# The first loads of a fused adaLN, linear attention and SwiGLU kernel, shared between the SyncE and ScalarE DMA queues

## The chip, the cores and the metric

The kernel runs on one core of one Trainium2 chip. The metric is the device time of one execution in microseconds (us), lower is better. Single executions of one kernel differ by one or two us in about 840. For each run the record gives the mean granted TensorE clock of the core (1.0 is full speed).

Engines are named as the profile names them: PE is TensorE, PEld its weight loads, DVE is VectorE, ACT is ScalarE, POOL is GpSimd, SP is SyncE. A "q" after an engine (SPq, ACTq) means its instruction sequencer, which also issues DMAs.

## The reference

One transformer block over 2048 tokens of width 1024. Only the head of it matters here: the modulation vectors come from a small condition vector `c` and the matrix `w_mod`, the input is normalised, scaled and shifted, and multiplied by the key weights.

```python
mod = (silu(c) @ w_mod).reshape(1, 6, 1, -1)          # w_mod: 1024 x 6144
sa, ca, ga, sb, cb, gb = mod[:, 0], ..., mod[:, 5]
h = layernorm(x) * (1 + ca) + sa                       # x: 2048 x 1024, bf16
x = x + ga * linear_attention(h, wqkv) @ wo
h = layernorm(x) * (1 + cb) + sb
x = x + gb * swiglu(h, w_gate, w_up, w_down)
```

## The kernel before

The kernel works on 512 tokens at a time. For the first 512 it must load four tiles of `x` (128 tokens each, 256 KB), `c`, four modulation blocks and eight key pieces (256 KB each) before it has everything for the key stage of these tokens. A modulation block `wme[b][q]` is 1 MB: half `b` of the columns for the scale (`q` = 1) or the shift (`q` = 0). All loads are issued by SyncE, in the order of need:

```python
    for st in range(STC - 1):                      # x tiles 0, 1, 2
        load_x(st, nc.sync)
    nc.sync.dma_start(out=c_sb[:], in_=c_v)
    ...
    def load_mod(b, q, lo, hi):
        nc.sync.dma_start(out=wme[b][q][:, :, lo:hi], in_=wm_v[:, :, q * D + b * NB + lo:q * D + b * NB + hi])
    def load_k(cc):
        nc.sync.dma_start(out=wk[cc // 4][:, cc % 4, :], in_=wqkv_v[:, cc, D:2 * D])

    load_mod(0, 1, 0, NB)
    load_mod(0, 0, 0, NB)
    load_k(0)
    load_k(1)
    load_x(STC - 1, nc.sync)
    load_k(2)
    load_k(3)
    load_mod(1, 1, 0, NB)
    load_mod(1, 0, 0, NB // 2)
    load_k(4)
    load_k(5)
    load_mod(1, 0, NB // 2, NB)
    load_k(6)
    load_k(7)
```

The head is written out by hand, with the order on DVE, ACT and POOL kept as written (`in_order`). PE keeps program order too. `keep_warm` issues dummy matmuls that only keep PE busy.

```python
    with in_order(nc.vector, nc.scalar, nc.gpsimd):
        ...
        nc.scalar.activation(out=scT[:], in_=mod_ps[:, 0:DC], func=ACT.Silu)
        xns = [ln1_norm(*ln1_stats(0, t)) for t in range(3)]     # normalised on ACT
        pe_transpose_tile(hT, xns[0], 0, DC)
        keep_warm(spare, 3)
        pe_transpose_tile(hT, xns[1], 1, DC)
        keep_warm(spare, 2)
        mod_block(0, 1, 0, 4)
        pe_transpose_tile(hT, xns[2], 2, DC // 2)                # half copied by ACT, half by DVE
        keep_warm(spare, 4)
        for lo, hi in ((0, 1), (1, 4)):
            mod_block(0, 0, lo, hi)
            for cc in range(lo, hi):
                modulate(hT, cc, ca1T, saT, 0, H)
        k_mms(0, gs, accs, 0, 4)                                 # the first key matmuls
        xn3 = ln1_norm(*ln1_stats(0, 3), dve=True)
        pe_transpose_tile(hT, xn3, 3, DC // 2)
        ...                                                      # block 1, the other key matmuls
```

`pe_transpose_tile(..., split)` lets ACT copy the column blocks from `split` on out of the transposed tile, and DVE the blocks before it. In the built program DVE's copy of a tile waits for ACT's copy of the same tile (tile 2: ACT from 11.78 to 12.36 us, DVE from 12.40).

In the built program of the changed kernel, the first 24 DMAs that SyncE and ScalarE issue take eight completion semaphores in rotation, over both queues together; the kernel before has such a rotation too. From the ninth on, a DMA waits, **on the engine that issues it**, for the DMA eight places earlier: in that trace each of the 16 issues begins after that DMA has landed, eleven of them within 0.02 us.

Of the kernel before, what the change touches and what calls it, by code (L numbers as in the profile page):

```python
# [21 lines left out]
def kernel(  # L22
# [13 lines left out]
    nc = tc.nc  # L36
    P = nc.NUM_PARTITIONS
    _, S, D = A_x.shape
# [4 lines left out]
    DC = D // P  # L43
# [4 lines left out]
    STC = SCW // P  # L48
    NB = 512
# [11 lines left out]
    wqkv_v = A_wqkv.rearrange("(c p) n -> p c n", p=P)  # L61
# [4 lines left out]
    wm_v = w_mod.rearrange("(j p) n -> p j n", p=P)  # L66
    c_v = c.rearrange("o (j p) -> (o j) p", p=P)
# [14 lines left out]
    @contextmanager  # L82
    def in_order(*engines):
        types = [e.engine for e in engines]
        traced = nc.cur_bb.bb.instructions
        mark = traced[-1]
        yield
        first = next(k for k in reversed(range(len(traced))) if traced[k] is mark) + 1
        for i in traced[first:]:
            if i.engine in types:  # L90
                prev = last_on.get(i.engine)
                if prev is not None:
                    tc.add_manual_dep(i, prev.name, mybir.DependencyInfo(
                        mybir.DependencyClass.NoSync, mybir.DependencyReason.DATA), reason="in_order")
                last_on[i.engine] = i

    def mm(out, lhsT, rhs, start, stop):
        return tc.keep_in_program_order(nc.tensor.matmul(out, lhsT=lhsT, rhs=rhs, start=start, stop=stop))  # L98

    def transpose(out, in_):  # L100
        return tc.keep_in_program_order(nc.tensor.transpose(out, in_, ident[:]))  # L101

    def big(name, shape):
        return k8.tile([P] + shape, BF16, name=name, tag="k8")
# [4 lines left out]
    def acc_b(name, shape=(NB,), dt=F32):  # L109
        return pb.tile([P] + list(shape), dt, name=name, tag="pb")  # L110
# [3 lines left out]
    c_sb = const.tile([DC, P], BF16, name="c_sb")  # L114
# [3 lines left out]
    def load_x(st, eng):  # L118
        x_sb = k2.tile([P, D], BF16, name="x_sb")
        eng.dma_start(out=x_sb[:], in_=x2[st * P:(st + 1) * P, :])  # L120
        x_tiles[st] = x_sb

    for st in range(STC - 1):
        load_x(st, nc.sync)
    nc.sync.dma_start(out=c_sb[:], in_=c_v)

    wk = [big("wk", [4, D]), big("wk", [4, D])]
    wme = [[big("wme", [DC, NB]) for _ in range(2)] for _ in range(2)]

    def load_mod(b, q, lo, hi):  # L130
        nc.sync.dma_start(out=wme[b][q][:, :, lo:hi], in_=wm_v[:, :, q * D + b * NB + lo:q * D + b * NB + hi])

    def load_k(cc):
        nc.sync.dma_start(out=wk[cc // 4][:, cc % 4, :], in_=wqkv_v[:, cc, D:2 * D])

    load_mod(0, 1, 0, NB)
    load_mod(0, 0, 0, NB)
    load_k(0)
    load_k(1)
    load_x(STC - 1, nc.sync)  # L140
    load_k(2)
    load_k(3)
    load_mod(1, 1, 0, NB)
    load_mod(1, 0, 0, NB // 2)
    load_k(4)
    load_k(5)
    load_mod(1, 0, NB // 2, NB)
    load_k(6)
    load_k(7)

    def load_w(view, lo, name):
        ts = []
# [42 lines left out]
    def rstd_of(mv, n):  # L195
        veps = small.tile([P, STC], F32, name="veps")
        nc.vector.tensor_scalar_add(out=veps[:, 0:n], in0=mv[:, 0:n, 1], scalar1=LN_EPS)  # L197
        rstd = small.tile([P, STC], F32, name="rstd")
        nc.gpsimd.tensor_tensor(out=rstd[:, 0:n], in0=veps[:, 0:n], in1=neg_half[:].to_broadcast([P, n]), op=ALU.pow)  # L199
        return rstd  # L200

    def bn(src, mv_out):
        stats = small.tile([P, NNB, nc.vector.BN_STATS_DIM], F32, name="stats")
        for i in range(NNB):
            nc.vector.bn_stats(out=stats[:, i, :], in_=src[:, i * NB:(i + 1) * NB])
        nc.vector.bn_aggr(out=mv_out, in_=stats[:])

    def normalise(dst, src, mean, rstd):
        nc.vector.tensor_scalar(out=dst, in0=src, scalar1=mean, scalar2=rstd, op0=ALU.subtract, op1=ALU.mult)

    def normalise_act(dst, src, mv, rstd):
        nmr = small.tile([P, 1], F32, name="nmr")
        nc.gpsimd.tensor_scalar(out=nmr[:], in0=mv[:, 0, 0:1], scalar1=rstd[:, 0:1], scalar2=-1.0,  # L213
                                op0=ALU.mult, op1=ALU.mult)
        nc.scalar.activation(out=dst, in_=src, func=ACT.Identity, bias=nmr[:], scale=rstd[:, 0:1])  # L215
# [5 lines left out]
    def pe_transpose_tile(hT, xn, t, split):  # L221
        tp = acc_b("tp", (DC, P), BF16)
        for cc in range(DC):
            transpose(tp[:, cc, :], xn[:, cc * P:(cc + 1) * P])
        if split < DC:
            nc.scalar.copy(out=hT[:, split:DC, t * P:(t + 1) * P], in_=tp[:, split:DC, :])  # L226
        nc.vector.tensor_copy(out=hT[:, 0:split, t * P:(t + 1) * P], in_=tp[:, 0:split, :])
# [3 lines left out]
    def ln1_stats(sc, t):  # L231
        x_sb = x_tiles.pop(sc * STC + t)
        mv = small.tile([P, STC, 2], F32, name="mv")
        bn(x_sb, mv[:, 0, :])
        rstd = rstd_of(mv, 1)
        return sc, t, x_sb, mv, rstd

    def ln1_norm(sc, t, x_sb, mv, rstd, dve=False):
        xn = k2.tile([P, D], BF16, name="xn", bufs=4)
        if dve:  # L240
            normalise(xn[:], x_sb[:], mv[:, 0, 0:1], rstd[:, 0:1])
        else:
            normalise_act(xn[:], x_sb[:], mv, rstd)
        if sc > 0:
            nc.sync.dma_start_transpose(hTs[sc][:, :, t * P:(t + 1) * P], xn[:])
        return xn
# [6 lines left out]
    def mod_block(b, q, lo, hi):  # L253
        for i in range(lo, hi):
            col = q * DC + 4 * b + i
            for j in range(DC):
                mm(mod_ps[:, col:col + 1], lhsT=wme[b][q][:, j, i * P:(i + 1) * P],
                   rhs=scT[:, j:j + 1], start=(j == 0), stop=(j == DC - 1))
        cs = slice(4 * b + lo, 4 * b + hi)
        src = mod_ps[:, q * DC + 4 * b + lo:q * DC + 4 * b + hi]  # L260
        if q == 1:
            nc.vector.tensor_scalar_add(out=ca1T[:, cs], in0=src, scalar1=1.0)
        else:
            nc.vector.tensor_copy(out=saT[:, cs], in_=src)
# [20 lines left out]
    def k_evac(sc, gs, accs):  # L285
        for (t, nb), acc in zip(gs, accs):
            phi_to(pks[sc][:, t, nb * NB:(nb + 1) * NB], acc[:])
# [125 lines left out]
    def keep_warm(acc, n):  # L413
        for _ in range(n):
            mm(acc[:], lhsT=sel[:, 0, :], rhs=sel[:], start=True, stop=True)
# [8 lines left out]
    with in_order(nc.vector, nc.scalar, nc.gpsimd):  # L424
        mod_ps = acc_b("mod_ps")
        mm(mod_ps[:, 0:DC], lhsT=c_sb[:], rhs=ident[0:DC, 0:DC], start=True, stop=True)
        keep_warm(spare, 10)
        nc.scalar.activation(out=scT[:], in_=mod_ps[:, 0:DC], func=ACT.Silu)
        xns = [ln1_norm(*ln1_stats(0, t)) for t in range(3)]
        pe_transpose_tile(hT, xns[0], 0, DC)  # L430
        keep_warm(spare, 3)
        pe_transpose_tile(hT, xns[1], 1, DC)
        keep_warm(spare, 2)
        mod_block(0, 1, 0, 4)
        pe_transpose_tile(hT, xns[2], 2, DC // 2)
# [5 lines that stand above are left out]
        k_mms(0, gs, accs, 0, 4)  # L441
        xn3 = ln1_norm(*ln1_stats(0, 3), dve=True)
        pe_transpose_tile(hT, xn3, 3, DC // 2)
        for cc in range(4):
            modulate(hT, cc, ca1T, saT, H, SCW)
        mod_block(1, 1, 0, 4)
        gs7, accs7 = k_groups[6:7], [acc_b("acc")]
        k_mms(0, gs7, accs7, 0, 2)
        for cc in (4, 5):
            mod_block(1, 0, cc - 4, cc - 3)  # L450
            modulate(hT, cc, ca1T, saT)
            if cc == 4:
                k_mms(0, gs7, accs7, 2, 4)
        k_mms(0, gs + gs7, accs + accs7, 4, 5)
        k_mms(0, gs[0:4], accs[0:4], 5, 6)
        mod_block(1, 0, 2, 4)
        for cc in (6, 7):
            modulate(hT, cc, ca1T, saT)
        k_mms(0, gs[4:6] + gs7, accs[4:6] + accs7, 5, 6)
        k_mms(0, gs + gs7, accs + accs7, 6, 8)  # L460
        gs8, accs8 = k_groups[7:8], [acc_b("acc")]
        k_mms(0, gs8, accs8)
        k_evac(0, gs, accs)
        k_evac(0, gs7, accs7)
        k_evac(0, gs8, accs8)
# [224 lines left out]
```

## Time and profile before

| | before |
|---|---|
| median of 3 runs | 839.66 us (838.86 to 839.79) |
| span of the profiled run | 836.6 us |
| PE busy | 829.8 us |
| first key matmul starts | 14.50 us |
| first v matmul starts (end of the key stage) | 31.95 us |

Three lines of the profile's page, from its parts 1 and 4: busy time of the engines, and the chain of work that ended last, by engine.

```profile
span 836.6 us, 11355 instructions
PE 829.8 (99%) x4701; PEld 380.7 (46%) x4701; DVE 307.6 (37%) x598; ACT 170.1 (20%) x255; POOL 60.9 (7%) x165
PE 97%; DMA 1%; DVE 1%; SPq 0%; ACT 0%; issue 0%
```

PE is the bound. The same chain in order of time (start, length, what) shows where it is not PE:

```profile
2.98 10.27 DMA wme<-in_w_mod_dram
...
14.64 5.20 PE acc L98 x24
...
27.19 36.00 PE acc L98 x166
```

Until 13.25 us the kernel waits for the first two modulation blocks, and from 27.19 us on it is matmuls without a gap.

The timeline of ACT in the head (start, length, engine, line, operation, and in brackets the idle time before it and what ended it):

```profile
9.39 1.24 ACT L215 ACTIVATE xn<-x_sb,nmr,rstd 128x1024 bf16<-128x1024 bf16 x1 [0.38 <-POOL nmr L213]
11.78 0.58 ACT L226 COPY hT<-tp 128x512 bf16<-128x512 bf16 x1 [1.15 <-PE tp L101]
20.33 0.58 ACT L226 COPY hT<-tp 128x512 bf16<-128x512 bf16 x1 [7.96 <-PE tp L101]
```

The second line is the copy of tile 2; the third is the copy of tile 3. PE, from the timeline:

```profile
14.50 5.34 PE L98 MATMUL acc<-wk,hT 128*128 128x512 bf16 x24
...
31.95 13.98 PE L98 MATMUL acc<-wv,hT 128*128 128x512 bf16 x64
```

And the head in stretches: window, its length, then busy us of each engine (instructions), the granted PE clock, DMA share and GB/s.

```profile
12.50:14.50 2.00, 1.06 (x33) 0.89 (x33) 0.86 (x3) 0.00 (x0) 0.00 (x0) 1.00 1.07 385
14.50:19.80 5.30, 5.30 (x33) 2.46 (x30) 3.22 (x9) 0.00 (x0) 2.04 (x34) 1.00 1.11 344
19.80:23.60 3.80, 2.90 (x62) 2.07 (x60) 2.13 (x9) 1.87 (x2) 0.13 (x1) 1.00 1.11 359
```

DMA's share is 1.07 to 1.11 throughout, at 344 to 385 GB/s. From 19.8 to 23.6 us PE does little: mostly small matmuls of one column (62 instructions in 2.90 us in all) and 0.90 us idle. The clock stays at 1.00.

### The profile page before, as it was taken

The page shows a single profiled execution, that of the slowest core. Times are in us where ns is not written, and L with a number is a line of the kernel's source. Part 1 is how long each engine was busy: PE and PEld are TensorE (multiplying, and loading weights), DVE is VectorE, ACT ScalarE, POOL GpSimd, SP SyncE. Part 2 cuts the span into 40 slices and gives each one's busy share as a digit, 9 for nine tenths or more (in the row PEclk, how much of TensorE's full clock was granted, in tenths as well). Part 3 has the DMA queues.
Part 4 walks back from the last instruction along what each step waited for, and adds up shares of the span by engine and source line. Part 5 has one row for each costly group of instructions (what it writes and reads, how often), then busy time and mean ns, then how long its engine had stood idle before and what let it go on. Part 6 is the DMA issues. An engine that isn't in the chain of part 4 may idle for free.

```text
span 836.6 us, 11355 instructions
## 1 busy us (share of the span) xinstructions
PE 829.8 (99%) x4701; PEld 380.7 (46%) x4701; DVE 307.6 (37%) x598; ACT 170.1 (20%) x255; POOL 60.9 (7%) x165
## 2 busy tenths in 40 slices
PE   8999999999999999999999999999999999999998
PEld 4444444444444444444444444444444444444444
DVE  5755554587413324521111344222114431111122
ACT  3455343334211111101111110111110101111000
POOL 2011211111130001100000010000001100000000
PEclk9999999999999999999999999999999999999999
DMA  9894890029997446337434173672505529710011
GB/s 311 305 253 100 254 213 2 13 68 239 366 243 262 151 151 207 120 99 229 150 102 151 45 221 100 201 239 62 189 1 127 188 69 322 241 60 0 13 64 51
DMA packets 127668, 129.34 MB, mean 155 GB/s; under 512 B 33920, under 2 KB 109184, under 8 KB 127104
## 3 DMA queue, kind: packets, MB, share of 16 engines
q1 hardware_dynamic: 123568, 115.36, 45.7%
q0 software_dynamic: 4048, 13.25, 5.4%
q8 instruction: 37, 0.61, 0.3%
q14 instruction: 15, 0.12, 0.1%
HBM read 108.53 MB, written 12.72 MB: 145 GB/s over the span
## 4 chain that ended last, share of the span: by engine, by line
PE 97%; DMA 1%; DVE 1%; SPq 0%; ACT 0%; issue 0%
PE acc L98 89%; PE a_ps L98 7%; DMA wme<-in_w_mod_dram 1%; PE kvp L98 1%; PE modr L98 0%; PE den L98 0%; PE mod_ps L98 0%; DVE hT L218 0%; SPq L120 0%; DVE wo L528 0%; PE wf L98 0%; DVE pq L273 0%; ACT eb L270 0%; ACT hT L226 0%; PE tp L101 0%
## 5 line engine op out<-in xcount | busy, mean ns | idle before, releaser
L98 PE MATMUL acc<-h2T,wgu 128*128 128x512 bf16 x1792 | 387.6, 379 | 0.0
L98 PEld LDWEIGHTS <-wgu 128*128 128x128 bf16 x1792 | 175.3, 98 | 211.3
L98 PE MATMUL acc<-wd,gu 128*128 128x512 bf16 (+2 forms) x924 | 196.1, 373 | 0.0
L597 DVE TENSOR_TENSOR gu<-acc,e 128x512 bf16<-128x512 f32 x112 | 77.5, 692 | 299.2 <-PE acc L98 296.5
L596 ACT ACTIVATE e<-acc 128x512 f32<-128x512 f32 x112 | 66.9, 597 | 374.8 <-PE acc L98 374.8
L98 PEld LDWEIGHTS <-gu 128*128 128x128 bf16 x924 | 89.3, 98 | 104.4
L98 PEld LDWEIGHTS <-hT 128*128 128x128 bf16 x512 | 49.2, 98 | 60.4 <-DVE hT L218 1.5
L618 DVE TENSOR_TENSOR e<-acc,gb_bc 128x512 f32<-128x512 f32 (+2 forms) x33 | 22.3, 675 | 131.9 <-PE acc L98 131.9
L98 PE MATMUL acc<-wk,hT 128*128 128x512 bf16 x256 | 57.6, 379 | 0.8 <-DVE hT L218 0.7
L98 PE MATMUL a_ps<-wo,pq 128*128 128x512 bf16 x256 | 57.4, 379 | 0.0
L98 PE MATMUL acc<-hT,wq 128*128 128x512 bf16 x256 | 56.8, 379 | 0.0
L98 PE MATMUL acc<-wv,hT 128*128 128x512 bf16 x256 | 55.9, 379 | 0.0
L270 ACT ACTIVATE eb<-acc 128x512 bf16<-128x512 f32 x64 | 37.9, 595 | 66.2 <-PE acc L98 63.1
L215 ACT ACTIVATE xn<-x,nmr,rstd 128x1024 bf16<-128x1024 f32 x16 | 19.8, 1240 | 126.3 <-POOL nmr L213 126.3
L565 POOL DMA_DIRECT2D x_scratch<-x x16 | 9.7, 608 | 418.5 <-DVE x L558 418.5
L98 PEld LDWEIGHTS <-pq 128*128 128x128 bf16 x256 | 25.0, 98 | 30.2
L98 PEld LDWEIGHTS <-wq 128*128 128x128 bf16 x256 | 24.6, 98 | 29.8 <-issue 0.9
L271 DVE TENSOR_SCALAR eb<-eb 128x512 bf16<-128x512 bf16 x64 | 18.4, 292 | 49.0 <-ACT eb L270 49.0
L558 DVE TENSOR_TENSOR x<-a_ps,x_sb 128x512 f32<-128x512 f32 x32 | 22.1, 691 | 7.9 <-PE a_ps L98 7.8
L199 POOL TENSOR_TENSOR rstd<-veps,neg_half 128x1 f32<-128x1 f32 x32 | 17.9, 559 | 75.3 <-DVE veps L197 72.9
L308 ACT CAST v<-acc 128x512 bf16<-128x512 f32 x32 | 18.3, 582 | 23.1 <-PE acc L98 23.0
L621 DVE TENSOR_TENSOR ob<-e,x1r 128x512 bf16<-128x512 f32 (+2 forms) x33 | 22.3, 675 | 1.0
(70 smaller groups left out, 263.1 us busy)
## 6 DMA issues: line engine op xcount, KB each, us to landing
wgu<-in_B_w_gate_dram SPq DMA_DIRECT2D x28, 1024.0 KB, 7.9
wgu<-in_B_w_up_dram SPq DMA_DIRECT2D x28, 1024.0 KB, 8.7
x_sb<-in_A_x_dram SPq DMA_DIRECT2D x32, 256.0 KB, 6.8
wml<-in_w_mod_dram SPq DMA_DIRECT2D x8, 1024.0 KB, 8.7
x_scratch<-x POOLq DMA_DIRECT2D x16, 512.0 KB, 3.0
x1r<-x_scratch SPq DMA_DIRECT2D x31, 256.0 KB, 2.8
wd<-in_B_w_down_dram SPq DMA_DIRECT2D x7, 1024.0 KB, 6.0
rbc<-rden_scratch POOLq DMA_DIRECT2D x16, 256.0 KB, 5.4
```

The lines of the kernel that those rows point to most:

```text
L98: return tc.keep_in_program_order(nc.tensor.matmul(out, lhsT=lhsT, rhs=rhs, start=start, stop=stop))
L199: nc.gpsimd.tensor_tensor(out=rstd[:, 0:n], in0=veps[:, 0:n], in1=neg_half[:].to_broadcast([P, n]), op=ALU.pow)
L215: nc.scalar.activation(out=dst, in_=src, func=ACT.Identity, bias=nmr[:], scale=rstd[:, 0:1])
L270: nc.scalar.activation(out=e[:], in_=acc, func=ACT.Exp)
L271: nc.vector.tensor_scalar(out=e[:], in0=e[:], scalar1=1.0, scalar2=PHI_EPS, op0=ALU.min, op1=ALU.add)
L308: nc.scalar.copy(out=v[:, t * D + nb * NB:t * D + (nb + 1) * NB], in_=acc[:])
L558: nc.vector.tensor_tensor(out=x1[:, ns], in0=a_ps[:], in1=x_t[:, ns], op=ALU.add)
L565: nc.gpsimd.dma_start(out=x1_dram[st * P:(st + 1) * P, :], in_=x1[:])
L596: nc.scalar.activation(out=sg[:], in_=ps[0][:], func=ACT.Silu)
L597: gm = nc.vector.tensor_tensor(out=guT[sc][f // GPT][:, f % GPT, :], in0=ps[1][:], in1=sg[:], op=ALU.mult)
L618: nc.vector.tensor_tensor(out=yt, in0=y_ps, in1=gb_bc[:, ns], op=ALU.mult)
L621: nc.vector.tensor_tensor(out=ob, in0=yt, in1=x1r, op=ALU.add)
```

## The change

The intent was to shorten the issue time at the head: two sequencers issue at the same time (in the trace of the changed kernel SyncE issues its half of the first block from 1.64 to 2.07 us and ScalarE its own from 1.74 to 2.19), and each modulation block comes in two halves, one from each queue. The two early blocks are shared at once. The second halves of the block-1 pieces are issued by ScalarE later, after its three normalisations.

```diff
-    for st in range(STC - 1):
-        load_x(st, nc.sync)
-    nc.sync.dma_start(out=c_sb[:], in_=c_v)
+    load_x(0, nc.sync)
+    load_x(1, nc.scalar)
+    load_x(2, nc.sync)
+    nc.scalar.dma_start(out=c_sb[:], in_=c_v)
...
+    def load_mod(b, q, lo, hi, eng, half):
+        js = slice(half * DC // 2, (half + 1) * DC // 2)
+        eng.dma_start(out=wme[b][q][:, js, lo:hi], in_=wm_v[:, js, q * D + b * NB + lo:q * D + b * NB + hi])
...
-    load_mod(0, 1, 0, NB)
-    load_mod(0, 0, 0, NB)
-    load_k(0)
-    load_k(1)
+    for q in (1, 0):
+        load_mod(0, q, 0, NB, nc.sync, 0)
+        load_mod(0, q, 0, NB, nc.scalar, 1)
+    load_k(0, nc.sync)
+    load_k(1, nc.scalar)
     load_x(STC - 1, nc.sync)
-    ... load_k(2) to load_k(7) and the block-1 loads, whole
+    ... the same with nc.sync, and only half 0 of each block-1 piece
...
         xns = [ln1_norm(*ln1_stats(0, t)) for t in range(3)]
+        load_mod(1, 1, 0, NB, nc.scalar, 1)
+        load_mod(1, 0, 0, NB // 2, nc.scalar, 1)
+        load_mod(1, 0, NB // 2, NB, nc.scalar, 1)
         pe_transpose_tile(hT, xns[0], 0, DC)
```

In the built program, the DMAs take their semaphores in this order (number, issuer, what, and for the late ones the number eight places back that they wait for):

```
 0 ACT c          8 ACT key 1                 16 SP  key 5                   -> waits for  8
 1 SP  x 0        9 SP  key 0                 17 SP  shift 1b, half 0        -> waits for  9
 2 ACT x 1       10 SP  x 3                   18 ACT scale 1,  half 1        -> waits for 10, x 3
 3 SP  x 2       11 SP  key 2                 19 SP  key 6                   -> waits for 11
 4 ACT scale 0   12 SP  key 3                 20 SP  key 7                   -> waits for 12
 5 SP  scale 0   13 SP  scale 1, half 0       21 ACT shift 1a, half 1        -> waits for 13, scale 1 half 0
 6 ACT shift 0   14 SP  shift 1a, half 0      22 SP  v weights               -> waits for 14
 7 SP  shift 0   15 SP  key 4                 23 ACT shift 1b, half 1        -> waits for 15, key 4
```

More of the change, by code (lines that the diff above doesn't have):

```diff
@@ L121, in load_x, with load_k @@
         x_tiles[st] = x_sb
-    for st in range(STC - 1):
-        load_x(st, nc.sync)
-    nc.sync.dma_start(out=c_sb[:], in_=c_v)
+    load_x(0, nc.sync)
+    load_x(1, nc.scalar)
+    load_x(2, nc.sync)
+    nc.scalar.dma_start(out=c_sb[:], in_=c_v)
     wk = [big("wk", [4, D]), big("wk", [4, D])]
     wme = [[big("wme", [DC, NB]) for _ in range(2)] for _ in range(2)]
-    def load_mod(b, q, lo, hi):
-        nc.sync.dma_start(out=wme[b][q][:, :, lo:hi], in_=wm_v[:, :, q * D + b * NB + lo:q * D + b * NB + hi])
-    def load_k(cc):
-        nc.sync.dma_start(out=wk[cc // 4][:, cc % 4, :], in_=wqkv_v[:, cc, D:2 * D])
-    load_mod(0, 1, 0, NB)
-    load_mod(0, 0, 0, NB)
-    load_k(0)
-    load_k(1)
-    load_x(STC - 1, nc.sync)
-    load_k(2)
-    load_k(3)
-    load_mod(1, 1, 0, NB)
-    load_mod(1, 0, 0, NB // 2)
-    load_k(4)
-    load_k(5)
-    load_mod(1, 0, NB // 2, NB)
-    load_k(6)
-    load_k(7)
+    def load_mod(b, q, lo, hi, eng, half):
+        js = slice(half * DC // 2, (half + 1) * DC // 2)
+        eng.dma_start(out=wme[b][q][:, js, lo:hi], in_=wm_v[:, js, q * D + b * NB + lo:q * D + b * NB + hi])
+    def load_k(cc, eng):
+        eng.dma_start(out=wk[cc // 4][:, cc % 4, :], in_=wqkv_v[:, cc, D:2 * D])
+    for q in (1, 0):
[3 more added lines that the diff above has]
+    load_k(1, nc.scalar)
+    load_x(STC - 1, nc.sync)
+    load_k(2, nc.sync)
+    load_k(3, nc.sync)
+    load_mod(1, 1, 0, NB, nc.sync, 0)
+    load_mod(1, 0, 0, NB // 2, nc.sync, 0)
+    load_k(4, nc.sync)
+    load_k(5, nc.sync)
+    load_mod(1, 0, NB // 2, NB, nc.sync, 0)
+    load_k(6, nc.sync)
+    load_k(7, nc.sync)
     def load_w(view, lo, name):
```

## The prediction

This was written before the changed kernel had run.

> **What bounds the kernel now.** TensorE. The page has PE 829.8 of 836.6 us busy, and the chain of waits is 97% PE. From 27.2 us on it is matmuls without a gap, so only the head can change. There the first modulation loads (`wme`) hold 2.98 to 13.25 us. The first k matmul starts at 14.5 us; from there the k stage takes 17.4 us with about 0.9 us of PE idle (windows of 1 us), and the v matmuls start at 31.95.
>
> **What the change does.** No arithmetic changes; the order of instructions on PE, DVE and POOL stays the same. Only DMA issues move.
> - Early part: x tile 1, c, halves of the first two modulation blocks and one key piece go to ScalarE's queue. SyncE issues cost 0.42 us each (timeline), and six precede the second block. DMA was already 0.77 to 1.09 busy from 2 us on, at 253 to 371 GB/s against 385 later. [...] My estimate from the rate dip: these blocks land 0.5 to 1 us sooner. Five issues come before ScalarE's table load (1.28 us);
> - Late part: three half pieces of block 1 are issued by ScalarE after the third `xn` activation (ends 10.63 us) and before the third `hT` copy (0.58 us, starts at 11.78). In the built order each of the three waits for an older DMA on a recycled semaphore: the first for x tile 3, the second for SyncE's half of the block-1 scale piece, the third for key piece 4. ScalarE runs in order, so the copy waits for all three; VectorE's copy of the same tile waits for ScalarE's.
>
> Landings in the trace: x tile 3 at 15.2, key piece 4 at 21.9 us. In the changed kernel 0.8 MB less stands before key piece 4 on its own queue (2.0 us at 385 GB/s), but the first ScalarE half, issued near 14.5 us, shares the engines with it (+1.4 us), and the ramp gains about 0.5. Estimate: key piece 4 lands at 20.3 us (19 to 21.7). Then issue 0.45, copy 0.58, VectorE copy 0.42, saT 0.16, the 24 remaining modulation matmuls 0.74 and gaps: the k matmuls start near 23 us instead of 14.5, **+8.5 us**, all on the critical path, since PE has nothing else in its order.
>
> PE then stands idle some 8 us. The first 11 matmuls of the trace took 4.24 us (0.385 each) against 0.233 for the next ten: an idle PE starts slow. I add **+1.5 us** for that. The early gain is lost, as the copy waits anyway.
>
> **Predicted: 849.5 us**, 845.5 to 853 (8 in 10). Faster by over 2%: 1%; within 2%: 95%; slower by over 2%: 4%.
>
> **What would show it.** ScalarE's third `hT` copy at 20.5 to 22.5 us; two or three ScalarE issues spread between 10.6 and 21 us, waiting for DMA; a PE gap of about 8 us before the first k matmul; that matmul at 22 to 24 us; the first k matmuls near 0.4 us each for 2 to 4 us; first two modulation blocks landed by 12 to 13 us; v matmuls at about 42 us; afterwards no gap and the same PE time.
>
> **What would make it wrong.** Key piece 4 landing before 16 us (a loss of a few us) or after 22 us (over 12). A PE that stays fast (1.5 us less). If the copy does not wait behind the issues: 838 to 839 us.

The sum came to +8.5 us for the wait and +1.5 us for the slow clock, 10 us on 839.66, about 849.5; the early gain in it (0.5 us off the landing of key piece 4) was the author's estimate from the rate dip. Two things that it takes as given are shown by the trace of the changed kernel. ScalarE kept its order: its copy of tile 2 ran at 20.21 us, behind the three issues, though its input was transposed by 11.5 us. And the two queues shared the DMA rate: from 7 to 12 us they moved 366 GB/s together, with a DMA share of 1.08, where SyncE's queue alone moved 361 in the trace of before, with 1.06.

## The result, and the profile after

The changed kernel took **848.51 us** (median of 4 runs, 847.71 to 848.85) against 839.26 us (838.16 to 839.79) for the kernel before beside it. The ratio is 1.0111, 95% interval 1.0093 to 1.0128: slower by 1.1%, which is clear of the noise and inside the 2% band that counts as the same. Ratios are the mean time of one kernel's fast runs over that of the other's of the same rounds, so not quite the ratio of the medians quoted.

The page of the changed kernel:

```profile
span 847.1 us, 11360 instructions
PE 832.3 (98%) x4701; PEld 381.5 (45%) x4701; DVE 307.7 (36%) x598; ACT 170.1 (20%) x255; POOL 60.7 (7%) x165
PE 96%; DMA 2%; DVE 1%; ACT 0%; ACTq 0%; issue 0%; SPq 0%
```

DMA's share of the chain rose from 1% to 2%, and ACTq, ScalarE's sequencer, is on it. The chain in order of time:

```profile
12.67 7.11 DMA wk<-in_A_wqkv_dram
...
19.80 0.37 ACTq L133
...
20.21 0.59 ACT hT L229
...
20.83 0.42 DVE hT L230
...
21.37 0.78 PE mod_ps L98 x24
22.16 6.58 PE acc L98 x24
...
37.45 36.00 PE acc L98 x166
```

A load of *key weights* (piece 4) now ends the wait of a *modulation* issue on ScalarE, behind which stand the copies, behind which stand PE's matmuls. The matmuls read none of that key piece at this point. The timeline of ACT:

```profile
9.52 1.24 ACT L218 ACTIVATE xn<-x_sb,nmr,rstd 128x1024 bf16<-128x1024 bf16 x1 [0.38 <-POOL nmr L216]
13.88 6.29 ACTq L133 DMA_DIRECT2D wme<-in_w_mod_dram  x3
20.21 0.58 ACT L229 COPY hT<-tp 128x512 bf16<-128x512 bf16 x1 [9.45 <-DMA wme<-in_w_mod_dram]
```

The copy of tile 2 is at 20.21 us instead of 11.78. Its three DMA issues, read one by one from the trace, begin just when the DMA landed that the table above says they wait for:

```
ScalarE issue at 13.88 us      x 3 landed at 13.86 us
ScalarE issue at 18.25 us      scale 1, half 0 landed at 18.23 us
ScalarE issue at 19.80 us      key 4 landed at 19.78 us
```

PE:

```profile
22.02 6.72 PE L98 MATMUL acc<-wk,hT 128*128 128x512 bf16 x24
...
42.21 13.98 PE L98 MATMUL acc<-wv,hT 128*128 128x512 bf16 x64
```

The key matmuls start 7.52 us later (22.02 against 14.50), and the v matmuls 10.26 us later (42.21 against 31.95): another 2.74 us are lost inside the key stage, by the same instructions. The stretches show why (the clock is the third number from the end):

```profile
12.50:21.40 8.90, 0.06 (x4) 0.02 (x1) 0.53 (x3) 0.58 (x1) 0.00 (x0) 0.62 1.09 374
21.40:24.50 3.10, 3.10 (x30) 1.48 (x30) 2.61 (x7) 0.00 (x0) 0.00 (x0) 0.50 1.06 390
24.50:28.70 4.20, 4.20 (x22) 1.94 (x21) 0.95 (x4) 0.00 (x0) 2.17 (x35) 0.96 1.07 405
28.70:32.60 3.90, 3.07 (x60) 2.04 (x58) 2.05 (x8) 1.87 (x2) 0.00 (x0) 0.88 1.05 404
32.60:35.00 2.40, 2.40 (x13) 0.90 (x11) 0.57 (x2) 0.00 (x0) 0.00 (x0) 0.50 1.05 409
```

After the gap the clock is at half, and the first 24 key matmuls take 6.72 us instead of 5.34. Then the thin stretch of one-column matmuls (19.8 to 23.6 us before), which went unpunished in the trace of before, is followed by a second period at half clock. From the first v matmul on, both kernels need the same time (847.1 - 42.21 = 804.9 us against 836.6 - 31.95 = 804.7).

### The profile page after: what moved, and what is told of

Its sections match the earlier page's. It is cut to its first block, busy times and chain, and to the rows that moved or that the text cites. A ratio compares the mean times of both kernels' runs of the same rounds, so it can differ in the third digit from the quotient of the medians.

```text
span 847.1 us, 11360 instructions
## 1 busy us (share of the span) xinstructions
PE 832.3 (98%) x4701; PEld 381.5 (45%) x4701; DVE 307.7 (36%) x598; ACT 170.1 (20%) x255; POOL 60.7 (7%) x165
## 3 DMA queue, kind: packets, MB, share of 16 engines
q0 software_dynamic: 4048, 13.25, 5.3%
## 4 chain that ended last, share of the span: by engine, by line
PE 96%; DMA 2%; DVE 1%; ACT 0%; ACTq 0%; issue 0%; SPq 0%
PE acc L98 88%; PE a_ps L98 7%; DMA wme<-in_w_mod_dram 1%; DMA wk<-in_A_wqkv_dram 1%; PE kvp L98 1%; PE modr L98 0%; PE den L98 0%; PE mod_ps L98 0%; DVE wo L534 0%; ACT hT L229 0%; PE wf L98 0%; DVE hT L221 0%; DVE hT L230 0%; ACTq L133 0%; DVE pq L276 0%
## 5 line engine op out<-in xcount | busy, mean ns | idle before, releaser
L98 PE MATMUL acc<-wk,hT 128*128 128x512 bf16 x256 | 60.6, 393 | 0.7 <-DVE hT L221 0.7
```

The source lines that it names most:

```text
L98: return tc.keep_in_program_order(nc.tensor.matmul(out, lhsT=lhsT, rhs=rhs, start=start, stop=stop))
```

## The experiments

Theory: ScalarE's copy of tile 2 stands behind three issues that wait for young DMAs; the delay is set by the landing of the DMA that the last of them waits for. Rivals: that splitting the pieces or sharing the engines between two queues slows the loads themselves; that any ScalarE issue before the copy costs the same; that the late halves' own landing is the cause, and the copy a bystander. The runs came in three groups, each on one chip with the kernel before beside it; all runs gave correct results.

### One part at a time

**The late halves back on SyncE** (the early part of the change kept):

```diff
+    load_mod(1, 1, 0, NB, nc.sync, 1)            # each right behind its half 0
...  (the same for the two shift pieces)
-        load_mod(1, 1, 0, NB, nc.scalar, 1)
-        load_mod(1, 0, 0, NB // 2, nc.scalar, 1)
-        load_mod(1, 0, NB // 2, NB, nc.scalar, 1)
```

> The early part of the change is kept; the three late half pieces of block 1 go back to SyncE, each right behind its other half, so nothing stands before ScalarE's copy of tile 2. If the loss is ScalarE's copy waiting behind those issues (my theory): the copy starts near 11.5 us again, the k matmuls near 13.5 to 14.5, no granted clock of 0.5, and the time is 838.3 us (837.5 to 839.5), i.e. 0 to 1.5 us below before. If splitting the pieces or sharing the engines between two queues is what costs (rival): it stays above 844.

Measured: 839.5 us (6 runs) against 839.39 for before, ratio 1.0003 (0.9989 to 1.0017). The whole loss is gone. The copy of tile 2 and the first key matmuls in this run:

```profile
12.04 0.59 ACT L232 COPY hT<-tp 128x512 bf16<-128x512 bf16 x1 [1.12 <-PE tp L101]
14.18 5.34 PE L98 MATMUL acc<-wk,hT 128*128 128x512 bf16 x23
```

The clock was 1.0 in the profiled run. The hoped-for gain of the early part did not show either.

**The late halves alone** (early loads whole and on SyncE, as before):

```diff
-    load_x(1, nc.scalar) ... load_k(1, nc.scalar)      # the early ScalarE issues
+    load_x(1, nc.sync)   ... load_k(1, nc.sync)        # as in the kernel before, blocks whole
```

> The late part alone: early loads whole and on SyncE as before, the three late halves on ScalarE before the copy of tile 2. In this build the three issues wait for x tile 2, the second modulation block and key piece 0, which in the trace of before landed at 6.2, 13.3 and 13.9 us, and not for x tile 3, the block-1 scale half and key piece 4. If the loss is set by which landing the issues wait for: the copy starts at 14.4 to 15.6 us, the k matmuls at 16 to 17.2, time 842 us (840.5 to 844). If any ScalarE issue before the copy costs the same whatever it waits for: 846 or more. If issuing alone costs nothing: 839.

Measured: 839.31 us, ratio 1.0004 (0.9988 to 1.002): nothing lost, less than expected. ACT in the timeline of this run:

```profile
9.60 2.77 ACTq L132 DMA_DIRECT2D wme<-in_w_mod_dram  x3
12.41 0.59 ACT L227 COPY hT<-tp 128x512 bf16<-128x512 bf16 x1 [1.58 <-DMA wk<-in_A_wqkv_dram]
```

The same three issues stand before the same copy, and the copy is only 0.6 us later than in the first trace of before. The order of semaphores differs in this build: the three issues wait for x tile 2, the second modulation block and key piece 0, the last of which landed at 11.98 us in this run. The expectation was too high because it took that landing from the trace of before (13.9 us); landings of the same loads vary by up to 2 us between runs (below). The same three issues on ScalarE were cheap (839.31 us) or dear (848.51) by **what they waited for**. Neither part alone costs anything that these runs can show (the intervals reach up to 0.2%, 1.7 us); together they do, because with the early part in place the built program has the late issues at places 18, 21 and 23 of the rotation instead of 10, 13 and 14, and eight places back from there stand DMAs that are still on their way (in the first trace they landed at 13.86, 18.23 and 19.78 us, when ScalarE had ended its normalisations at 10.76).

### The copy taken out from behind the issues

```diff
-        pe_transpose_tile(hT, xns[2], 2, DC // 2)
+        pe_transpose_tile(hT, xns[2], 2, DC)        # the changed kernel, tile 2 copied by DVE alone
```

> The changed kernel, with the whole copy of tile 2 given to VectorE: all DMA issues stay as they are. If the copy behind the issues is the cause, the k matmuls start at 13 to 14.5 us instead of 22.0; but the late halves still land at 22.0, 25.7 and 29.0 us, and the block-1 modulation matmuls, at 20.1, 22.5 and 25.9 us in before, have to wait for them, so not all comes back: 843 us (841 to 845.5). If the late landing alone is the cause (rival): 847 or more. If the copy alone is: 838 to 840.

Measured: 841.71 us against 839.39, ratio 1.0031 (1.0015 to 1.0047). Same DMAs, same issues, same waits, and most of the loss is gone. What is left is named by the timeline (its first line is the start of the key matmuls):

```profile
14.51 5.34 PE L98 MATMUL acc<-wk,hT 128*128 128x512 bf16 x23
20.86 0.59 ACT L229 COPY hT<-tp 128x512 bf16<-128x512 bf16 x1 [9.94 <-DMA wk<-in_A_wqkv_dram]
22.31 0.39 PE L98 MATMUL acc<-wk,hT 128*128 128x512 bf16 x1 [1.23 <-DVE hT L221]
23.80 0.25 PE L98 MATMUL mod_ps<-scT,wme 128*128 128x1 bf16 x4 [0.52 <-DMA wme<-in_w_mod_dram]
24.76 4.05 PE L98 MATMUL acc<-wk,hT 128*128 128x512 bf16 x11
```

The copy of tile 3 is now the first one behind the issues (it ran at 20.86 us, though PE had transposed its input by 20.30; the last issue waited for key piece 4, landed at 20.43); PE then waits 0.52 us for a late half; and the eleven matmuls after that run at half clock (4.05 us instead of 2.55). So the late landing costs something, but little: the blocked copy of tile 2 was the main cause.

### One, two or three late issues

The first chip group was followed by one on another chip, with the changed kernel again, and with only the first, or the first two, of the late halves left on ScalarE.

```diff
         load_mod(1, 1, 0, NB, nc.scalar, 1)
-        load_mod(1, 0, 0, NB // 2, nc.scalar, 1)    # one late issue: both of these on SyncE
-        load_mod(1, 0, NB // 2, NB, nc.scalar, 1)   # two: only this one
```

> The changed kernel with only the first of the three late halves on ScalarE, the other two on SyncE behind their other halves. That one issue waits for x tile 3, which landed at 13.1 to 13.9 us so far. If the copy of tile 2 follows the landing that the last issue before it waits for: the copy starts at 13.5 to 14.4, the k matmuls at 15.3 to 16.2, time 841 us (840 to 842.5).

> As before it, with the first two late halves on ScalarE. The second waits for SyncE's half of the block-1 scale piece, which landed at 16.6 to 18.2 us so far. If the copy follows the last landing waited for: the copy starts at 17 to 18.8, the k matmuls at 18.7 to 20.6, time 845 us (843.5 to 847), between one late issue (841) and three (848.5). If the loss came from the number of transfers that share the engines, it would rise from one to two to three by equal steps of about 3 us, whatever lands when.

The changed kernel, unchanged, and the kernel before, unchanged, on that chip:

> The changed kernel, unchanged, for more runs beside before on one chip. The granted clock is given in windows of 3.41 us; in 11 runs of before, 4 had a mean clock of 1.0 (838.0 us on average) and 7 of 0.998, one window at half speed (839.8). If the second half-clock window of the changed kernel is a matter of where the windows fall, its runs should again split in two groups, 0.994 and 0.992, about 1 to 2 us apart; the time 848.5 us (847.7 to 849.3).

> The kernel before, unchanged, for a second trace of it on the chip of this batch. In its first trace the first modulation block landed at 10.3 us and the second at 13.3; the run with the late part alone, whose early loads are the same, had them at 8.3 and 11.3 on another chip. If the early landing differs by 2 us from run to run, this trace may show either; the copy of tile 2 should start at 11 to 12 us and the k matmuls at 14 to 14.6 in both cases.

Measured (times in us from the traces; the time is the median; before was 838.53 in this group, 839.39 in that of the first row):

| late issues on ScalarE | last one waits for | landed | copy of tile 2 | first key matmul | first v matmul | time |
|---|---|---|---|---|---|---|
| none | - | - | 12.04 | 14.18 | 31.62 | 839.5 |
| one | x tile 3 | 13.73 | 14.27 | 16.06 | 36.31 | 841.6 |
| two | scale 1, half 0 | 16.82 | 17.25 | 19.05 | 39.11 | 846.21 |
| three (the change) | key piece 4 | 18.25 | 18.68 | 20.49 | 40.72 | 848.96 |

The copy starts 0.43 to 0.54 us after the landing in each row: one issue, then the copy. Two ACT lines, with one and with two late issues:

```profile
14.27 0.58 ACT L231 COPY hT<-tp 128x512 bf16<-128x512 bf16 x1 [3.44 <-DMA x_sb<-in_A_x_dram]
```

```profile
17.25 0.58 ACT L230 COPY hT<-tp 128x512 bf16<-128x512 bf16 x1 [6.32 <-DMA wme<-in_w_mod_dram]
```

The steps in time are 2.1, 4.6 and 2.8 us (the first is 3.0 if each time is taken against the before of its own group). They do not follow the landings alone (the first key matmul moves by 1.9, 3.0 and 1.4 us); in the traces the rest is slow clock in the key stage, which takes 17.4 us in the first row and 20.1 to 20.3 in the others. The times alone would hardly tell these steps from the equal ones of about 3 us that sharing the engines was expected to give; what tells is the copy, which follows the landing in each row. With one late issue the profiled run, the slowest of its four, had a clock of 0.996, so its v matmuls came late for its median.

The ratio of the changed kernel on this chip was 1.0123 (1.0104 to 1.0143). Its profiled run had the second thin stretch at full clock; its clock was 0.994. The kernel before, profiled again, had the copy at 12.27 (expected at 11 to 12) and the key matmuls at 14.13 us.

### The clock

Each trace gives the granted clock in periods at 1.0 or 0.5, with nothing between; all but the last, which the end of the trace cuts, are multiples of 3.41 us long (10.24, 10.24, 6.83, 3.41 and 812.37 us in the first trace of the changed kernel; the last of these is 238 times 3.41). In that trace the key matmuls start 0.43 us apart at 0.5 (from 22.40 us) and 0.22 apart at 1.0 (from 25.12). The records begin only 3.9 to 6.8 us into the run; a clock of 1.00 printed for the time before that says nothing (in the first trace of before, where they begin at 4.67 us, the first 11 matmuls took 4.24 us and the next ten 2.33). Where the periods start, relative to the kernel, differs from run to run (the first one recorded at 4.67 us in the first trace of before, at 4.37 in that of the changed kernel). This fits a thin stretch that is punished or not by where it falls in the periods, but no trace of a slow-clock run of before was kept, so for that kernel it is not shown. By mean clock the runs fall into groups:

| kernel | runs with the higher clock | runs with one more half-clock period |
|---|---|---|
| before (29 runs of the three groups) | 18 at 1.0, mean 838.01 us | 11 at 0.998, mean 839.89 us |
| changed (8 runs) | 4 at 0.994, mean 848.13 us | 4 at 0.992, mean 849.01 us |

The two groups of before differ by 1.9 us; 3.41 us at half speed would be worth 1.7. Those of the changed kernel differ by only 0.9 us: there, how much of the half-clock time falls into the idle gap, where it costs nothing, differs as well. Its two traces, one of each group, need the same 20.2 us for the key stage.

PE's busy time in a period does not by itself tell whether the clock drops after it. It dropped after a period with PE busy for 1.30 of 3.40 us (the copy moved to DVE, 21.00 to 24.40 us), and after one with 2.59 of 3.42 us, much of it one-column matmuls (the changed kernel, 28.26 to 31.68 us). Yet it did not drop after one with 1.93 of 3.41 us (36 dummies, the run below, 11.35 to 14.76 us).

To see what the first, long gap costs by its clock, dummies were put into it, in the changed kernel:

```diff
             mod_block(0, 0, lo, hi)
+            if lo == 0:
+                keep_warm(spare, 36)
             for cc in range(lo, hi):
```

> The changed kernel with 36 more dummy matmuls (0.216 us each, 7.8 us) in the PE gap from 12.5 to 21.4 us, so that PE stays busy there. The k matmuls should start at 22 us as before it, but the granted clock should stay at 1.0 throughout, the first 24 of them take 5.3 us instead of 6.7, and the second stretch of half clock near 32 to 35 us should go too: 846.2 us (845 to 847.3). If the slow clock costs nothing on the critical path: 848.5.

Measured: 847.75 us (846.41 to 849.29). Two windows of the profiled run: the first 24 key matmuls, and the later half-clock period.

```profile
22.40:27.70 5.30, 5.25 (x31) 2.46 (x30) 3.23 (x9) 0.00 (x0) 2.04 (x35) 1.00 1.06 399
31.90:35.20 3.30, 3.30 (x9) 1.22 (x8) 0.10 (x1) 0.00 (x0) 0.00 (x0) 0.50 1.05 402
```

The time is above the expected range (845 to 847.3). The first part of the expectation held, 5.34 us for the first key matmuls; the second did not. The half-clock period behind the thin stretch comes without a slow clock in the long gap, and it came in two of four runs (848.91 us on average, against 846.69 in the two without). The dummies also ended late in the profiled run, at 21.94 us, as the second block landed later than in the first trace. So fewer were tried:

```diff
-                keep_warm(spare, 36)
+                keep_warm(spare, 26)
```

> The changed kernel with 26 dummies (5.6 us) in the PE gap instead of 36, so that they end before VectorE is released near 20 to 21 us. The first gap then has full clock throughout, the second stretch of half clock may come or not: mean clocks 1.0 and 0.998 instead of 0.994 and 0.992, the first 24 k matmuls 5.3 us instead of 6.7 to 8.1, and 846.6 us (845.5 to 847.7) against 848.7 of the changed kernel, 1.5 to 2.5 us less.

Measured: 848.87 us, ratio to before 1.012 (1.0101 to 1.0139), with before at 838.1 on this third chip. This missed: key piece 4 landed at 19.76 us, so the dummies left a gap of 2.5 us, and the clock was cut again in the profiled run. The four runs are 846.23 us (clock 1.0), 848.19 (0.998), 849.56 and 849.99 (0.996): one half-clock period more, some 1.8 us more. Filling the gap does not recover the loss; its larger part is the wait.

Last, the thin stretch in the kernel *before*, the likely place of the half-clock period that 11 of its 29 runs have. Three or six dummies of 0.19 us were put on PE after the transposes of tile 3:

```diff
         pe_transpose_tile(hT, xn3, 3, DC // 2)
+        for _ in range(3):      # or 6
+            mm(mod_ps[:, 64:NB], lhsT=sel[:, 0, :], rhs=..., start=True, stop=True)   # unused columns
```

> The kernel before with three dummy matmuls (448 columns, 0.19 us each) put after the transposes of tile 3, where PE has 0.7 us idle a little later. Before has, in 11 of 18 runs seen by now beside other kernels, one clock window at half speed (mean clock 0.998 instead of 1.0) and is about 1.8 us slower in them. If that window is cut because PE did too little in it: fewer or no runs at 0.998, and 838.0 us (837.5 to 838.8) against about 839 for before. If the dummies only lengthen the path: 839.5 or more.

> The same with six dummies, 1.1 us: more than the idle 0.7 us, so up to 0.5 us on the path, but no run should be left with a half-speed window: 838.4 us (837.8 to 839.3).

(The first of these says 11 of 18; counted again, it was 10 of 18.) Measured: 838.08 us with three (ratio 0.9997, 0.9984 to 1.001) and 838.14 with six (0.9995, 0.9983 to 1.0008). All 11 runs had a clock of 1.0, and their means, 838.16 and 838.02 us, are those of the full-clock runs of before. But before had only one half-clock run in 11 on this chip, so that there was none in these 11 proves nothing: that the dummies remove the bad case is not shown. No version beat both kernels by a difference that the runs can show.

### What the split did to the loads

The early part was meant to bring the first blocks sooner. The landing of the second modulation block (both halves), in all traces:

| early loads | landed at, us |
|---|---|
| whole, SyncE alone (5 traces) | 13.25, 12.26, 11.30, 12.02, 12.21 |
| halves, both queues (8 traces) | 12.23, 12.92, 13.04, 13.37, 13.85, 13.33, 13.14, 12.89 |

No gain: on average the block was even later (13.1 against 12.2 us), though the ranges overlap. In the split form SyncE's half landed at 10.7 to 11.8 us and ScalarE's at 12.2 to 13.9: 0.5 to 3.0 us after it. The block is complete only with the later one. The second queue added no rate once DMA was busy: from 7 to 12 us DMA moved 361 GB/s in the first trace of before and 366 in that of the changed kernel. Some time was saved before that: from 4 to 5 us DMA moved 202 to 253 GB/s in four of the five traces with whole loads (321 in the fifth) and 279 to 366 in the eight split ones, and x tile 3 landed at 13.6 us on average instead of 14.2. But the second block did not get it: SyncE's next loads went beside the half that PE was waiting for (in the run with the late halves on SyncE, key piece 0 landed at 12.17 us, before ScalarE's half of the block at 13.04).

## Why the prediction was right

- **What bounds the kernel:** right. The head alone changed; from the first v matmul on, the two profiled runs differ by 0.2 us.
- **The blocked copy:** right, and shown four ways. The issues begin 0.02 us after the landings they wait for; with the issues elsewhere the loss is gone (839.5 us); with the copy elsewhere most of it is gone (841.71); with one and two issues the copy follows each landing. ScalarE kept its order in the trace: the copy's input was transposed by 11.5 us, and it ran at 20.21, behind the issue at 19.80.
- **The delay of the first key matmul:** +8.5 us predicted, +7.5 measured in the first pair of traces and +6.4 in the second (20.49 against 14.13). Key piece 4 landed at 19.78 and 18.25 us, where the estimate had 20.3 (19 to 21.7): a term that was too large, and one that varies by 1.5 us from run to run. The steps from there to the first key matmul were oversized too: 2.7 us in the estimate, 2.24 in both traces.
- **The slow clock:** +1.5 us predicted, 2.7 measured in both pairs (42.21 - 22.02 = 20.19 and 40.72 - 20.49 = 20.23 us for the key stage, against 17.45). Undersized. In the first trace the estimate covered the half clock after the gap (1.4 us) but not a second half-clock period at the thin stretch (about 1.2 us on eleven matmuls that took 3.73 us instead of 2.55). In the second trace there was no second period, but the first 24 matmuls lost 2.8 us: there PE began again at 19.85 us, within the period from 19.34 to 22.75 us, and the clock stayed at half for the rest of it and for the whole period after it (the key matmuls ran at half from 20.49 to 26.16 us, half of which is the 2.8).
- **The sum:** +10 us predicted, +9.25 by the medians. The two terms above erred in opposite directions, so it is partly luck that the sum came this close. The profiled spans differ by 10.5 us, more than the medians, because the profiled run of before was one with full clock and that of the changed kernel one with the second half-clock period.
- **The early gain of 0.5 to 1 us:** wrong, in a step on which only 0.5 us of the estimate for key piece 4 rested. The first pair of traces seems to show it (12.23 against 13.25 us), but over 13 traces the split blocks landed no sooner. The rate dip that it was read from is real, and the split form fills it (see above); wrong was that the blocks would get the time saved, when each is complete only with the later of its halves. (Five SyncE issues precede the second block's, not six.)

What stays open: why landings of the same loads differ by up to 2 us between runs; what in a period makes the clock drop (PE's busy time does not by itself tell it, see the section on the clock); and whether the dummies in the thin stretch are worth anything on average.

## What to carry to other kernels

Here a DMA issue stood in the issuing engine's order like any other instruction, and where its semaphore was a recycled one, it waited for another DMA that had nothing to do with its data (a 0.58 us copy ran at 20.21 instead of 11.78 us, behind a modulation issue that waited for key piece 4 until 19.78). So before moving an issue to a compute engine, count back in the built program to the DMA it will wait for, and look at what stands behind it in that engine's order. Two parts of a change may each be free and still cost together (839.5 and 839.31 us apart, 848.51 together), here because one moved the other's place in the rotation; test them apart before giving up both. Where PE is the bound as it is here, count a PE gap as its length plus half of the time that then runs at half clock (2.8 and 5.7 us at half clock in the two traces of the changed kernel, with key matmuls 0.43 instead of 0.22 us apart in the first), and compare runs of the same mean clock before reading anything into 2 us (before: 838.01 us on average at 1.0, 839.89 at 0.998).
